# Lightning attention and a SwiGLU FFN in one kernel: an FFN that opens on two blocks, equal weight pieces, and DMA transposes issued with their loads

## The chip, the cores and the metric

The kernel runs on one core of one Trainium2 chip. The metric is device time in microseconds of one execution. Durations of single instructions come from one profiled execution.

## The reference, cut to what matters

There are 4 sequences of 768 tokens, 8 heads of 64, and a decay `lam` per head. Attention is linear with decay; the reference goes over blocks of 64 tokens and carries a state `kv` per head:

```python
intra = (q_b @ k_b.T * Dmask) @ v_b               # inside the block
inter = (q_b * lam_pow) @ kv                      # what came before it
out_b = intra + inter
kv = lam**block * kv + (k_b * rev_pow).T @ v_b
```

The output, seen as x of 3072 tokens by 512, goes through the FFN, with weights of 512 x 1536, 512 x 1536 and 1536 x 512:

```python
g = x @ w_gate
y = (g * sigmoid(g) * (x @ w_val)) @ w_out        # float32, 3072 x 512
```

## The kernel before, in words

**Tiling.** The kernel uses blocks of 128 tokens: 6 per sequence, N = 24 in all. The heads are kept as four pairs (HP), so one block is 128 x 512. The FFN works on tiles of blocks, `TILES`: tile 0 has blocks 0 to 3, tiles 1 and 2 have two blocks each (4 and 5, 6 and 7), and tiles 3 to 6 have four blocks each. The 1536 hidden columns are 12 steps (`fc`) of 128.

**Loads.** `load_kq(n)` loads k and q of a block on the queue of GpSimd (POOL), which turns float32 into bf16 on the way; `load_v(n)` loads v as float32. SyncE (SP) loads lambda, k and q of block 0, and v of the first `FIRST` blocks. Weights w_gate and w_val come in pieces whose widths, in units of 128 columns, are in `PIECES`; `load_w(c)` loads one piece of both, `load_wo(c)` a quarter of w_out. All of them are issued by POOL.

**Attention of a block** is four helpers:
- `scale_v(n)` multiplies v by the reversed decay, on POOL.
- `transposes(n)` gives kT and qT. For n under `PE_T` = 8, TensorE (PE) transposes into PSUM, ScalarE (ACT) copies k, and VectorE (DVE) multiplies q by the decay `qscale`. From block 8 on it is one DMA transpose of k and q together, issued by SP (L184).
- `scores(n)` multiplies kT and qT on PE (L207); DVE multiplies by the mask into `ssb` (L213).
- `cluster(n, n2)` is the rest: the state's part `kv_bd` x qT (L221), then `scores(n2)` if one is named, then `v_s` x `ssb` (L227), the copy into `xT` (L232 on ACT, or L234 on DVE from block 8 on), and the state's update: `up` on PE (L240), `kv_st` on DVE, its bf16 copy `kv_bd` in two halves (ACT for n under `PE_T`, L251; POOL from then on, L253), and `kv_dec`, the decayed state (DVE, then POOL).

**FFN.** `fc_mms(tt, fc, lo, hi)` does the four matmuls of gate and the four of value of one step on the columns lo to hi of a tile (L273). `ffn_fc` adds Silu on ACT (L286) and the product with the value on DVE into `h_sb` (L289). `ffn_out(tt, sub)` does 12 matmuls with w_out for one block (L297), copies on ACT (L300) and stores through SP (L301).

**Buffers that matter.** PSUM pool `ps_f` has 4 buffers, shared by gate, value, PE transposes and, from block 8 on, `up`. `ps_o` has 2 (attention outputs and FFN outputs) and `ps_s` has 1 (scores). Loads of k and q have 10 buffers, v 9, `v_s` 4, `qkT` 6.

**Order.** `tc.manual_schedule()` keeps the order of the program text on every engine, so that each engine is a queue with its instructions in the order in which the helpers are called. POOL issues a DMA when its place in that order comes; in the trace it has at most eight loads of its own under way. `keep_warm` puts matmuls without use into gaps of the opening. In the opening, attention of blocks 0 to 3 is interleaved with loads of weights; then tile 0 opens: its first two steps run on three blocks (`LAST`), while block 3 is finished, and then on the fourth. Blocks 4 to 7 are computed between the steps of tiles 0 and 1. From tile 2 on there is one block for every three steps, in three positions `pos`:

```python
if pos == 0:   scores(8) once; scale_v(n + 1); transposes(n + 3)
elif pos == 1: cluster(n, n + 1)
elif pos == 2: load(n + 6); ffn_out(*outs.pop(0))
```

The FFN outputs run behind: while tile 2 is computed, tile 0 is put out, and four outputs are left for the end.

Of the kernel before, what the change touches and what calls it, by code (L numbers as in the profile page):

```python
# [9 lines left out]
BF16 = mybir.dt.bfloat16  # L10
AF = mybir.ActivationFunctionType
# [11 lines left out]
def kernel(  # L23
# [20 lines left out]
    MC = DM // 128  # L44
    FC = DFF // 128
    TT = 512
    FIRST = 4
    PE_T = 8

    TILES = [(0, 4), (4, 2), (6, 2)] + [(i, 4) for i in range(8, N, 4)]  # L50
    PIECES = [1, 2, 3, 3, 3]
    PIECE_OF = [(c, f) for c, w in enumerate(PIECES) for f in range(w)]
    OPC = 3

# [21 lines left out]
    def load_v(n, eng):  # L76
        b, j = divmod(n, NB)
        v_raw[n] = vpool.tile([128, H, D], FP32, name="v_raw", tag="v_raw")
        eng.dma_start(out=v_raw[n], in_=v5[b, j])  # L79

    def load_kq(n):
        b, j = divmod(n, NB)
        t = ld.tile([128, 2, H, D], BF16, name="kq_nat", tag="kq")
        nc.gpsimd.dma_start(out=t[:, 0], in_=k5[b, j])  # L84
        nc.gpsimd.dma_start(out=t[:, 1], in_=q5[b, j])  # L85
        k_nat[n], q_nat[n] = t[:, 0], t[:, 1]
        state["kq", n] = t

    def load(n):
        load_kq(n)  # L90
        load_v(n, nc.gpsimd)

    wg_sb, wv_sb, wo_sb = {}, {}, {}
    wg_r = moe_w_gate.rearrange("(c p) f -> p c f", p=128)
# [44 lines left out]
                   allow_small_or_imprecise_dtypes=True)  # L139
    causal = const.tile([128, 128], BF16, name="causal")  # L140
    make_upper_triangular(nc, causal, val=1.0, diag=True)
    load_kq(1)
    load_kq(2)

# [13 lines left out]
    lamb = const.tile([128, HP], FP32, name="lamb")  # L158
    nc.scalar.activation(lamb, ln_all[:, H:H + HP], AF.Exp, scale=float(BLK))

    kv_bd = []
    for i in range(2):
        t = const.tile([128, HP, 128], BF16, name=f"kv_bd{i}")
        nc.vector.memset(t, 0.0)
        kv_bd.append(t)
    mask = const.tile([128, 2, HP, BLK], BF16, name="mask")
    nc.vector.tensor_tensor(out=mask, in0=bap(causal, [[0, 2], [0, HP], [1, BLK]]),
                            in1=bap(invb, [[1, 2], [2, HP], [0, BLK]]), op=ALU.mult)
# [47 lines left out]
    def cluster(n, scores_of=None):  # L216
        j = n % NB
        op = ps_o.tile([128, HP, BLK], FP32, name="op", tag="o")
        if j > 0:
            for p in range(HP):  # L220
                nc.tensor.matmul(op[:, p, :], kv_bd[n % 2][:, p, :], qT[n][:, p, :],  # L221
                                 start=(p == 0), stop=False, skip_group_check=True)
        if scores_of is not None:
            scores(scores_of)
        for p in range(HP):
            for h2 in range(2):
                nc.tensor.matmul(op[64 * h2:64 * h2 + 64, p, :], v_s[n][:, 2 * p + h2, :],  # L227
                                 ssb[n][:, h2, p, :], start=(j == 0 and p == 0), stop=(p == HP - 1),
                                 skip_group_check=True)
        x = xT[:, :, n * BLK:(n + 1) * BLK]  # L230
        if n < PE_T:
            nc.scalar.copy(out=x, in_=op)  # L232
        else:
            nc.vector.tensor_tensor(out=x, in0=op, in1=qscale, op=ALU.mult)  # L234
        if j < NB - 1:
            up = (ps_o if n < PE_T else ps_f).tile([128, HP, D], FP32, name="up",
                                                    tag="o" if n < PE_T else "f")
            for p in range(HP):
                for h2 in range(2):
                    nc.tensor.matmul(up[64 * h2:64 * h2 + 64, p, :], k_nat[n][:, 2 * p + h2, :],  # L240
                                     v_s[n][:, 2 * p + h2, :], start=True, stop=True)
            st = apool.tile([128, HP, D], FP32, name="kv_st", tag="kv_st")
            if j == 0:
                nc.vector.tensor_copy(out=st, in_=up)
            else:
                nc.vector.tensor_tensor(out=st, in0=state.pop("dec"), in1=up, op=ALU.add)  # L246
            bd = kv_bd[(n + 1) % 2]
            for h2 in range(2):
                r = slice(64 * h2, 64 * h2 + 64)
                if n < PE_T:  # L250
                    nc.scalar.copy(out=bd[r, :, 64 * h2:64 * h2 + 64], in_=st[r])  # L251
                else:
                    nc.gpsimd.tensor_copy(out=bd[r, :, 64 * h2:64 * h2 + 64], in_=st[r])  # L253
            if j < NB - 2:
                dec = apool.tile([128, HP, D], FP32, name="kv_dec", tag="kv_dec")
                (nc.vector if n < PE_T else nc.gpsimd).tensor_tensor(
                    out=dec, in0=st, in1=bap(lamb, [[1, HP], [0, D]]), op=ALU.mult)
                state["dec"] = dec
        del ssb[n], v_s[n], k_nat[n], kT[n], qT[n]
# [16 lines left out]
            if i == 0 and gate_done is not None:  # L276
                gate_done()

    def ffn_fc(tt, fc, lo=0):
        nt = TILES[tt][1] * BLK  # L280
        if tt not in h_sb:
            h_sb[tt] = hpool.tile([128, FC, TT], BF16, name="h_sb", tag="h")
        sil = fpool.tile([128, TT], BF16, name="sil", tag="sil")

        def silu():
            nc.scalar.activation(sil[:, 0:nt], gv[tt, fc][0][:, 0:nt], AF.Silu)  # L286

        fc_mms(tt, fc, lo, nt, silu)
        nc.vector.tensor_tensor(out=h_sb[tt][:, fc, 0:nt], in0=sil[:, 0:nt],  # L289
                                in1=gv.pop((tt, fc))[1][:, 0:nt], op=ALU.mult)  # L290

    def ffn_out(tt, sub):
        t0 = (TILES[tt][0] + sub) * BLK
        op = ps_o.tile([128, DM], FP32, name="yp", tag="o")
        for fc in range(FC):
            c, f = divmod(fc, OPC)
            nc.tensor.matmul(op, h_sb[tt][:, fc, sub * 128:(sub + 1) * 128], wo_sb[c][:, f, :],  # L297
                             start=(fc == 0), stop=(fc == FC - 1))
        osb = fpool.tile([128, DM], FP32, name="osb", tag="osb")
        nc.scalar.copy(out=osb, in_=op)  # L300
        nc.sync.dma_start(out=out[t0:t0 + 128, :], in_=osb)  # L301


    primed = const.tile([128, HP], FP32, name="primed")
    transposes(0)
    scale_v(0)
    load_kq(3)
    keep_warm(3)
    scores(0)
    scale_v(1)  # L310
    load_w(0)
    keep_warm(5)
    cluster(0)
    transposes(1)
    nc.scalar.activation(primed, lamb, AF.Silu)
    keep_warm(2)
    scores(1)
    scale_v(2)
    load_w(1)
    keep_warm(4)  # L320
    transposes(2)
    cluster(1)
    keep_warm(1)
    scores(2)
    scale_v(3)
    load_w(2)
    keep_warm(4)
    cluster(2)
    transposes(3)
    load_w(3)  # L330
    keep_warm(3)
    scores(3)


    LAST = (FIRST - 1) * BLK
    fc_mms(0, 0, 0, LAST)
    cluster(3)
    fc_mms(0, 1, 0, LAST)
    ffn_fc(0, 0, LAST)
    ffn_fc(0, 1, LAST)  # L340
    load(4)
    load_w(4)
    load(5)
    for fc in range(2, FC):
        ffn_fc(0, fc)
        if fc == 3:
            load(6)
        elif fc == 5:
            load(7)
        elif fc == 7:  # L350
            scale_v(4)
            transposes(4)
            for c in range(2):
                load_wo(c)
        elif fc == 8:
            scores(4)
            scale_v(5)
            for c in range(2, 4):
                load_wo(c)
        elif fc == 9:  # L360
            cluster(4)
            transposes(5)
        elif fc == 10:
            scores(5)
            load(8)


    fc_mms(1, 0, 0, BLK)
# [1 line left out]
    fc_mms(1, 1, 0, BLK)  # L370
    ffn_fc(1, 0, BLK)
    ffn_fc(1, 1, BLK)
    load(9)
    scale_v(6)
    transposes(6)
    for fc in range(2, FC):
        ffn_fc(1, fc)
        if fc == 2:
            scores(6)
            scale_v(7)  # L380
            load(10)
        elif fc == 5:
            transposes(7)
            transposes(8)
        elif fc == 6:
            cluster(6, 7)
            load(11)
            scale_v(8)
        elif fc == 8:
            cluster(7)  # L390
            load(12)
        elif fc == 9:
            transposes(9)
            load(13)
    transposes(10)


    outs = [(0, s) for s in range(4)] + [(1, 0), (1, 1), (2, 0), (2, 1)]
    outs += [(tt, s) for tt in range(3, len(TILES)) for s in range(4)]
    for tt in range(2, len(TILES)):  # L400
        for per in range(4):
            n = 4 * (tt - 2) + 8 + per
            for pos in range(3):
                ffn_fc(tt, 3 * per + pos)
                if pos == 0:
                    if n == 8:
                        scores(8)
                    if n + 1 < N:
                        scale_v(n + 1)
                    if n + 3 < N:  # L410
                        transposes(n + 3)
                elif pos == 1:
                    if n < N:
                        cluster(n, n + 1 if n + 1 < N else None)
                elif pos == 2:
                    if n + 6 < N:
                        load(n + 6)
                    ffn_out(*outs.pop(0))
    for o in outs:
        ffn_out(*o)  # L420
# [31 lines left out]
```

## Time and profile before

| what | value |
|---|---|
| median of 13 runs | 245.65 us (242.23 to 247.16) |
| the profiled execution | 245.0 us; the span of its instructions 243.2 us |
| granted TensorE clock over the span | 0.991 |
| PE, PEld, DVE, ACT, POOL busy | 95%, 50%, 43%, 33%, 46% |
| HBM read, written | 28.32 MB, 6.29 MB |
| a matmul step of 512 columns (8 matmuls) | 1.73 us |
| an output of one block (12 matmuls) | 2.59 us |
| a load of k, of q, of v, issue to landing (medians) | 7.0, 7.5, 8.1 us |
| a DMA transpose, issue to landing (median of 16) | 7.4 us |

The page gives the busy time of each engine, the same in 40 slices of 6.1 us, the DMA queues, the chain of work that ended last, the costliest groups of instructions, and the DMA issues. In a timeline row the columns are start and duration in us, engine, line, operation, output and input, the number of instructions, and in brackets the idle time of the engine before it with what ended it. SPq marks SP's queue, where waiting and issuing count and no work is done. A busy PE is not PE at its peak, since matmuls overlap.

### The profile page before, as it was taken

To read this page: it belongs to the slowest core of one execution; us is meant where nothing else is said; L and a number is where in the kernel's file an instruction comes from. 1 tells how busy PE (TensorE), PEld (TensorE's weight loads), DVE (VectorE), ACT (ScalarE), POOL (GpSimd) and SP (SyncE) were. 2 spreads that over 40 slices of the span, in tenths; PEclk is the share of its full clock that TensorE was granted. 3 is DMA by queue.
4 is the path that set the end of the run, shared out by engine and by line. 5 is a ranking of instruction groups with operands and counts; after the bars stand their busy time and mean duration, and the time that the engine had idled before them with its cause. 6 is when DMAs were issued, how large, how long until landed. Compare 5 with 4: busy or idle time off the path is not lost.

```text
span 243.2 us, 4289 instructions
## 1 busy us (share of the span) xinstructions
PE 230.3 (95%) x1712; PEld 122.7 (50%) x1712; DVE 104.3 (43%) x168; ACT 79.5 (33%) x152; POOL 111.9 (46%) x150
## 2 busy tenths in 40 slices
PE   8898999999299999999999999999999999999993
PEld 3465445787257764455455444445545444444441
DVE  2874545675345543454355256246246322322200
ACT  6565445447002222213213213222221222232121
POOL 8599559999445892745834940331231000000000
PEclk9999999999979999999999999999999999999999
DMA  7999999999999999899779893513100110111022
GB/s 122 194 145 187 207 201 221 203 210 140 157 162 153 185 135 166 165 133 154 74 119 156 93 186 86 67 23 88 46 9 34 46 43 0 43 46 43 24 105 86
DMA packets 83075, 28.32 MB, mean 116 GB/s; under 512 B 73072, under 2 KB 78704, under 8 KB 83056
## 3 DMA queue, kind: packets, MB, share of 16 engines
q0 software_dynamic: 56320, 16.00, 67.6%
q1 hardware_dynamic: 26736, 12.07, 26.7%
q8 instruction: 13, 0.21, 0.4%
q14 instruction: 6, 0.05, 0.1%
HBM read 28.32 MB, written 6.29 MB: 142 GB/s over the span
## 4 chain that ended last, share of the span: by engine, by line
PE 89%; DMA 5%; ACT 2%; DVE 2%; issue 1%; ACTq 0%; DVEq 0%
PE yp L297 26%; PE gp L273 26%; PE vp L273 24%; DMA qkT<-kq_nat 5%; PE op L227 3%; PE sp L207 3%; PE warm_ps L126 2%; PE tp L193 2%; PE op L221 2%; PE up L240 1%; DVE ssb L213 1%; ACT xT L232 1%; ACT kv_bd L251 1%; ACT qkT L195 0%; DVE qkT L196 0%
## 5 line engine op out<-in xcount | busy, mean ns | idle before, releaser
L289 DVE TENSOR_TENSOR h_sb<-sil,vp 128x512 bf16<-128x512 bf16 (+1 forms) x84 | 51.0, 611 | 108.0 <-PE vp L273 92.8
L273 PE MATMUL gp<-xT,wg 128*128 128x512 bf16 (+3 forms) x352 | 77.2, 342 | 0.2
L273 PE MATMUL vp<-xT,wv 128*128 128x512 bf16 (+3 forms) x352 | 77.1, 342 | 0.0
L286 ACT ACTIVATE sil<-gp 128x512 bf16<-128x512 f32 (+1 forms) x84 | 44.7, 536 | 80.6 <-PE gp L273 74.8
L297 PE MATMUL yp<-wo,h_sb 128*128 128x512 bf16 x288 | 66.5, 383 | 0.0
L273 PEld LDWEIGHTS <-wv 128*128 128x128 bf16 x352 | 33.9, 98 | 29.1
L297 PEld LDWEIGHTS <-h_sb 128*128 128x128 bf16 x288 | 28.5, 99 | 34.0 <-issue 1.4
L273 PEld LDWEIGHTS <-wg 128*128 128x128 bf16 x352 | 31.7, 98 | 27.6 <-issue 0.5
L253 POOL CAST kv_bd<-kv_st 64x256 bf16<-64x256 f32 x26 | 10.2, 393 | 63.8 <-DVE kv_st L246 47.7
L300 ACT COPY osb<-yp 128x512 f32<-128x512 f32 x24 | 14.1, 586 | 65.8 <-PE yp L297 65.8
L213 DVE TENSOR_TENSOR ssb<-sp,mask 128x1024 bf16<-128x1024 f32 (+1 forms) x28 | 29.5, 1066 | 7.2 <-PE sp L207 7.0
L177 POOL TENSOR_TENSOR v_s<-v_raw,rev 128x512 bf16<-128x512 f32 x24 | 25.6, 1070 | 3.2 <-DMA v_raw<-in_v_dram 3.0
L84 POOL DMA_DIRECT2D kq_nat<-in_k_dram x23 | 21.4, 932 | 2.1 <-DMA kq_nat<-in_k_dram 1.2
L85 POOL DMA_DIRECT2D kq_nat<-in_q_dram x23 | 20.5, 893 | 2.6 <-DMA wg<-in_moe_w_gate_dram 1.5
L79 POOL DMA_DIRECT2D v_raw<-in_v_dram x20 | 18.2, 912 | 2.9 <-DMA kq_nat<-in_k_dram 2.2
L207 PE MATMUL sp<-qkT 64*128 64x128 bf16 x192 | 9.5, 219 | 7.0 <-DMA qkT<-kq_nat 5.0
L207 PEld LDWEIGHTS <-qkT 64*128 64x128 bf16 x192 | 5.5, 94 | 12.4 <-DMA qkT<-kq_nat 5.4
L126 PE MATMUL warm_ps<-warm 128*128 128x512 bf16 x32 | 10.4, 459 | 1.2 <-DVE warm L121 1.2
L234 DVE TENSOR_TENSOR xT<-op,qscale 128x512 bf16<-128x512 f32 x16 | 10.9, 681 | 0.0
L227 PE MATMUL op<-ssb,v_s 128*64 128x128 bf16 x192 | 10.1, 225 | 0.5 <-DVE ssb L213 0.5
L221 PE MATMUL op<-qkT,kv_bd 128*128 128x128 bf16 x80 | 7.7, 219 | 0.3 <-ACT kv_bd L251 0.3
L227 PEld LDWEIGHTS <-v_s 128*64 128x64 bf16 x192 | 6.1, 109 | 3.5 <-POOL v_s L177 0.7
(47 smaller groups left out, 89.5 us busy)
## 6 DMA issues: line engine op xcount, KB each, us to landing
out_dram<-osb SPq DMA_DIRECT2D x24, 256.0 KB, 2.2
v_raw<-in_v_dram POOLq DMA_DIRECT2D x20, 256.0 KB, 8.1
kq_nat<-in_k_dram POOLq DMA_DIRECT2D x23, 128.0 KB, 7.0
kq_nat<-in_q_dram POOLq DMA_DIRECT2D x23, 128.0 KB, 7.5
wo<-in_moe_w_out_dram POOLq DMA_DIRECT2D x4, 384.0 KB, 7.4
wg<-in_moe_w_gate_dram POOLq DMA_DIRECT2D x3, 384.0 KB, 7.7
wv<-in_moe_w_val_dram POOLq DMA_DIRECT2D x3, 384.0 KB, 8.9
v_raw<-in_v_dram SPq DMA_DIRECT2D x4, 256.0 KB, 7.4
```

Of the source, the lines that this page charges most:

```text
L79: eng.dma_start(out=v_raw[n], in_=v5[b, j])
L84: nc.gpsimd.dma_start(out=t[:, 0], in_=k5[b, j])
L85: nc.gpsimd.dma_start(out=t[:, 1], in_=q5[b, j])
L126: nc.tensor.matmul(warm_ps, warm[:, 0:128], warm, start=True, stop=True)
L177: nc.gpsimd.tensor_tensor(out=t, in0=v_raw.pop(n), in1=bap(rev, [[1, H], [0, D]]), op=ALU.mult)
L207: nc.tensor.matmul(sp[:, h2, p, :], kT[n][r, p, :], qT[n][r, p, :], start=True, stop=True)
L213: nc.vector.tensor_tensor(out=s[:, :, ps], in0=sp[:, :, ps], in1=mask[:, :, ps], op=ALU.mult)
L227: nc.tensor.matmul(op[64 * h2:64 * h2 + 64, p, :], v_s[n][:, 2 * p + h2, :], ssb[n][:, h2, p, :], start=(j == 0 and p == 0), stop=(p == HP ...
L273: nc.tensor.matmul(gv[tt, fc][i][:, lo:hi], w[c][:, mc, fs], xT[:, mc, t0 + lo:t0 + hi], start=(mc == 0), stop=(mc == MC - 1))
L286: nc.scalar.activation(sil[:, 0:nt], gv[tt, fc][0][:, 0:nt], AF.Silu)
L289: nc.vector.tensor_tensor(out=h_sb[tt][:, fc, 0:nt], in0=sil[:, 0:nt], in1=gv.pop((tt, fc))[1][:, 0:nt], op=ALU.mult)
L297: nc.tensor.matmul(op, h_sb[tt][:, fc, sub * 128:(sub + 1) * 128], wo_sb[c][:, f, :], start=(fc == 0), stop=(fc == FC - 1))
```

## The change

- `FIRST` becomes 3, so SP loads v of blocks 0 to 2 only; k, q and v of block 3 are loaded by POOL between weight pieces. The weight pieces become six of 256 columns.
- The zeroing of `kv_bd` moves from DVE to POOL, ahead of POOL's first load. The Silu table is loaded (`primed`) before block 1's transposes instead of after them.
- Tile 0 opens after scores(2): step 0 on blocks 0 and 1, then cluster(2), then step 1 on two blocks, then both on block 2; steps 2 to 5 on three blocks, with block 3's attention between them; then steps 0 to 5 on block 3 alone, and steps 6 to 11 on all four. `ffn_fc` gets a range of columns for this.
- For blocks from 8 on, `load` issues the DMA transpose right after the loads, so SP's queue has the transposes in the order of the loads. Loads are called four blocks ahead of the cluster instead of six, and `transposes` is no longer called three blocks ahead.
- In tile 2 the four clusters stand at other places: scores(8) after the first output, cluster(8) after step 3, cluster(9) after the second output, cluster(10) after step 7, cluster(11) after step 10. `scale_v` and the loads follow the clusters.
- Stores of the output are issued by ACT instead of SP.
- The bf16 copies of the state for blocks 8 to 11 go from POOL to ACT.

```diff
-    FIRST = 4
+    FIRST = 3
-    PIECES = [1, 2, 3, 3, 3]
+    PIECES = [2] * 6
 def load(n):
     load_kq(n)
     load_v(n, nc.gpsimd)
+    if n >= PE_T:
+        transposes(n)
...
+    for i in range(2):                      # ahead of load_kq(1), load_kq(2)
+        t = const.tile([128, HP, 128], BF16, name=f"kv_bd{i}")
+        nc.gpsimd.memset(t, 0.0)            # was nc.vector.memset, later
...
-                if n < PE_T:
+                if n < 12:
                     nc.scalar.copy(out=bd[r, :, 64 * h2:64 * h2 + 64], in_=st[r])
...
-        nc.sync.dma_start(out=out[t0:t0 + 128, :], in_=osb)
+        nc.scalar.dma_start(out=out[t0:t0 + 128, :], in_=osb)
```

The opening and tile 2, as they stand after the change:

```python
transposes(0); scale_v(0); load_w(0); keep_warm(3); scores(0)
scale_v(1); load_w(1); keep_warm(4); cluster(0)
nc.scalar.activation(primed, lamb, AF.Silu); keep_warm(4)
transposes(1); scale_v(2); load(3); keep_warm(2); scores(1)
load_w(2); keep_warm(2); transposes(2); cluster(1)
load_w(3); keep_warm(1); scores(2)
A, B3 = 2 * BLK, 3 * BLK
fc_mms(0, 0, 0, A); cluster(2); fc_mms(0, 1, 0, A)
ffn_fc(0, 0, A, B3); ffn_fc(0, 1, A, B3)
scale_v(3); load_w(4); ffn_fc(0, 2, 0, B3); load_w(5)
transposes(3); ffn_fc(0, 3, 0, B3); load(4)
scores(3); ffn_fc(0, 4, 0, B3); load(5)
cluster(3); ffn_fc(0, 5, 0, B3); load(6)
for fc in range(6):
    ffn_fc(0, fc, B3, 4 * BLK, B3)
for fc in range(6, FC):
    ffn_fc(0, fc)          # after 8: scale_v(4), load(7); after 9: transposes(4), scale_v(5)
...                        # after 10: scores(4), transposes(5), load_wo(0), load_wo(1)
cluster(4); scores(5)
...                        # tile 1: load(8) after step 2, load(9) after 5, load(10) after 8, load(11) after 10
for per in range(4):                       # tile 2
    for pos in range(3):
        ffn_fc(2, 3 * per + pos)
        if pos == 2:
            ffn_out(*outs.pop(0))
        if (per, pos) == (0, 2):
            scores(8)
        elif (per, pos) == (1, 0):
            cluster(8, 9); scale_v(10); load(12)
        elif (per, pos) == (1, 2):
            cluster(9, 10); scale_v(11); load(13)
        elif (per, pos) == (2, 1):
            cluster(10, 11); scale_v(12); load(14)
        elif (per, pos) == (3, 1):
            cluster(11, 12); scale_v(13); load(15)
```

In tiles 3 to 6 the cluster stays at position 1, now with `scale_v(n + 2)` and `load(n + 4)` right behind it, and the output at position 2.

More of the change, by code (lines that the diff above doesn't have):

```diff
@@ L141 @@
     make_upper_triangular(nc, causal, val=1.0, diag=True)
+    kv_bd = []
+    for i in range(2):
+        t = const.tile([128, HP, 128], BF16, name=f"kv_bd{i}")
+        nc.gpsimd.memset(t, 0.0)
+        kv_bd.append(t)
     load_kq(1)
@@ L159 @@
     nc.scalar.activation(lamb, ln_all[:, H:H + HP], AF.Exp, scale=float(BLK))
[L161 to L165, printed above, removed]
     mask = const.tile([128, 2, HP, BLK], BF16, name="mask")
@@ L277, in fc_mms, with ffn_fc @@
                 gate_done()
-    def ffn_fc(tt, fc, lo=0):
-        nt = TILES[tt][1] * BLK
+    def ffn_fc(tt, fc, lo=0, hi=None, frm=0):
+        hi = TILES[tt][1] * BLK if hi is None else hi
         if tt not in h_sb:
@@ L283, in ffn_fc @@
         sil = fpool.tile([128, TT], BF16, name="sil", tag="sil")
+        cs = slice(frm, hi)
         def silu():
[L286 to L290, printed above, removed]
+            nc.scalar.activation(sil[:, cs], gv[tt, fc][0][:, cs], AF.Silu)
+        fc_mms(tt, fc, lo, hi, silu)
+        nc.vector.tensor_tensor(out=h_sb[tt][:, fc, cs], in0=sil[:, cs],
+                                in1=gv.pop((tt, fc))[1][:, cs], op=ALU.mult)
     def ffn_out(tt, sub):
@@ L306 @@
     scale_v(0)
-    load_kq(3)
+    load_w(0)
     keep_warm(3)
@@ L310 @@
     scale_v(1)
-    load_w(0)
-    keep_warm(5)
+    load_w(1)
+    keep_warm(4)
     cluster(0)
+    nc.scalar.activation(primed, lamb, AF.Silu)
+    keep_warm(4)
     transposes(1)
-    nc.scalar.activation(primed, lamb, AF.Silu)
+    scale_v(2)
+    load(3)
     keep_warm(2)
     scores(1)
-    scale_v(2)
-    load_w(1)
-    keep_warm(4)
+    load_w(2)
+    keep_warm(2)
     transposes(2)
     cluster(1)
+    load_w(3)
     keep_warm(1)
     scores(2)
+    A, B3 = 2 * BLK, 3 * BLK
+    fc_mms(0, 0, 0, A)
+    cluster(2)
+    fc_mms(0, 1, 0, A)
+    ffn_fc(0, 0, A, B3)
+    ffn_fc(0, 1, A, B3)
     scale_v(3)
-    load_w(2)
-    keep_warm(4)
-    cluster(2)
+    load_w(4)
+    ffn_fc(0, 2, 0, B3)
+    load_w(5)
     transposes(3)
-    load_w(3)
-    keep_warm(3)
+    ffn_fc(0, 3, 0, B3)
+    load(4)
     scores(3)
-    LAST = (FIRST - 1) * BLK
-    fc_mms(0, 0, 0, LAST)
+    ffn_fc(0, 4, 0, B3)
+    load(5)
     cluster(3)
[L338 to L344, printed above, removed]
+    ffn_fc(0, 5, 0, B3)
+    load(6)
+    for fc in range(6):
+        ffn_fc(0, fc, B3, 4 * BLK, B3)
+    for fc in range(6, FC):
         ffn_fc(0, fc)
-        if fc == 3:
-            load(6)
-        elif fc == 5:
+        if fc == 8:
+            scale_v(4)
             load(7)
-        elif fc == 7:
-            scale_v(4)
+        elif fc == 9:
             transposes(4)
-            for c in range(2):
-                load_wo(c)
-        elif fc == 8:
+            scale_v(5)
+        elif fc == 10:
             scores(4)
[L357 to L361, printed above, removed]
             transposes(5)
-        elif fc == 10:
-            scores(5)
-            load(8)
+            load_wo(0)
+            load_wo(1)
+    cluster(4)
+    scores(5)
     fc_mms(1, 0, 0, BLK)
@@ L372 @@
     ffn_fc(1, 1, BLK)
-    load(9)
     scale_v(6)
-    transposes(6)
+    load_wo(2)
+    load_wo(3)
     for fc in range(2, FC):
@@ L378 @@
         if fc == 2:
+            transposes(6)
+            scale_v(7)
+            load(8)
+        elif fc == 3:
             scores(6)
-            scale_v(7)
-            load(10)
         elif fc == 5:
             transposes(7)
-            transposes(8)
+            load(9)
         elif fc == 6:
             cluster(6, 7)
-            load(11)
             scale_v(8)
@@ L390 @@
             cluster(7)
[L391 to L395, printed above, removed]
+            load(10)
+        elif fc == 10:
+            load(11)
+            scale_v(9)
     outs = [(0, s) for s in range(4)] + [(1, 0), (1, 1), (2, 0), (2, 1)]
     outs += [(tt, s) for tt in range(3, len(TILES)) for s in range(4)]
-    for tt in range(2, len(TILES)):
+    for per in range(4):
+        for pos in range(3):
+            ffn_fc(2, 3 * per + pos)
+            if pos == 2:
+                ffn_out(*outs.pop(0))
+            if (per, pos) == (0, 2):
+                scores(8)
+            elif (per, pos) == (1, 0):
+                cluster(8, 9)
+                scale_v(10)
+                load(12)
+            elif (per, pos) == (1, 2):
+                cluster(9, 10)
+                scale_v(11)
+                load(13)
+            elif (per, pos) == (2, 1):
+                cluster(10, 11)
+                scale_v(12)
+                load(14)
+            elif (per, pos) == (3, 1):
+                cluster(11, 12)
+                scale_v(13)
+                load(15)
+    for tt in range(3, len(TILES)):
         for per in range(4):
-            n = 4 * (tt - 2) + 8 + per
+            n = 4 * tt + per
             for pos in range(3):
                 ffn_fc(tt, 3 * per + pos)
[L405 to L414, printed above, removed]
+                if pos == 1 and n < N:
+                    cluster(n, n + 1 if n + 1 < N else None)
+                    if n + 2 < N:
+                        scale_v(n + 2)
+                    if n + 4 < N:
+                        load(n + 4)
                 elif pos == 2:
-                    if n + 6 < N:
-                        load(n + 6)
                     ffn_out(*outs.pop(0))
```

## The prediction

> **What bounds the kernel now.** I read the page first (busy shares, slices, the chain of work that ended last), then the waits, then the timeline around the two places where TensorE (PE) stands still.
>
> ```profile
> PE   8898999999299999999999999999999999999993
> PEclk9999999999979999999999999999999999999999
> PE 89%; DMA 5%; ACT 2%; DVE 2%; issue 1%; ACTq 0%; DVEq 0%
> ```
>
> PE carries 89% of the chain: nearly all the rest of the kernel is matmuls back to back, and only idle PE time can be won. The one large hole is the slice marked 2 (61 to 67 us), with the only clock digit under 9 right behind it. The share of 5% for DMA names the cause; cut into stages by hand:
>
> ```profile
> 16.00:20.05 4.05, 2.90 (x42) 1.68 (x40) 2.38 (x5) 2.18 (x5) 4.05 (x7) 1.00 1.25 148
> 20.05:44.36 24.31, 24.30 (x189) 12.83 (x185) 12.99 (x20) 10.91 (x20) 18.97 (x24) 1.00 1.57 205
> 44.36:60.84 16.48, 15.94 (x201) 13.05 (x199) 10.04 (x22) 9.32 (x22) 16.35 (x19) 1.00 1.60 182
> 60.84:68.20 7.36, 2.41 (x45) 1.90 (x46) 2.35 (x4) 0.38 (x1) 2.64 (x3) 1.00 1.77 152
> ```
>
> Columns: stretch, length, then busy us of PE, PEld, DVE, ACT, POOL, granted clock, DMA share. Tile 0 of the FFN (20.05 to 44.36) is full; 60.84 to 68.20 has 2.41 us of matmul in 7.36, so **4.95 us idle**. The timeline names who ends it:
>
> ```profile
> 53.12 14.64 SPq L184 DMA_TRANSPOSE qkT<-kq_nat  x4
> 62.38 0.40 PE L207 MATMUL sp<-qkT 64*128 64x128 bf16 x8 [1.54 <-DMA qkT<-kq_nat]
> 67.39 0.40 PE L207 MATMUL sp<-qkT 64*128 64x128 bf16 x8 [3.41 <-DMA qkT<-kq_nat]
> ```
>
> scores(8) and scores(9) wait for the first two DMA transposes (1.54 + 3.41 = 4.95). I call the transpose of block n T(n) and its loads L(n). T8 is issued at 53.12, as soon as q of block 8 has landed (44.23 + 8.8 us to landing), and takes 9.2 us more; T9 takes 11.7, T10 12.5, T11 11.5, T12 7.8. The DMA row of the page is at 9 from the second slice to the sixteenth, so the rings are a queue and what is late is late by its place in it.
>
> The other place is the start:
>
> ```profile
> 2.06 1.07 POOL L84 DMA_DIRECT2D kq_nat<-in_k_dram  x1
> 12.33 1.28 ACT L315 ACT_TABLE_LOAD   x1
> 12.37 0.40 PE L207 MATMUL sp<-qkT 64*128 64x128 bf16 x8 [1.01 <-ACT qkT L195]
> 19.72 0.40 PE L207 MATMUL sp<-qkT 64*128 64x128 bf16 x8 [0.85 <-ACT qkT L195]
> 20.05 0.82 PE L273 MATMUL gp<-xT,wg 128*128 128x384 bf16 x4
> ```
>
> The first FFN matmul runs at 20.05, behind scores(3).
>
> **What the skill says.** "TensorE: Matmul & The Clock Gate" (Part 1) says that an idle window of some 3.4 us puts the PE clock to half. The trace agrees in kind: after the waits of 1.54 and 3.41 us the granted clock averages 0.86 over 68 to 80 us, 12 x 0.14 = **1.7 us** lost. "DMA: Bandwidth & Descriptors" (Issuing engines are not separate DMA queues) says that moving a DMA to another issuing engine saves only issue time; the trace shows SP's v loads and POOL's k and q loads landing in turn, so stores on ACT cost the rings what they did. "Perfetto Trace Analysis" (DMA Instruction — HWDGE) says that one descriptor generator serves both hardware-issuing engines under a lock. Before, only SP uses it; no run here shows it contended. I use it for a rival.
>
> **The change, part by part.** Loads land in order. In the saturated stretch k, q and v follow each other by some 0.9 us, a weight piece of 384 columns takes 1.9, of 256 columns 1.3, a piece of w_out 1.95.
>
> *Start.* The two memsets of kv_bd go from VectorE (DVE, 0.55 us for both, hidden there) to POOL, ahead of its first load. POOL's 128x128 memset took 0.20 and a one-column one 0.10; four times the columns gives an estimate of 0.5 each, so POOL's first load starts at 3.1 instead of 2.1. v of block 3 leaves SP's queue, which gives back the same 1 us of ring: q of block 1 lands near 10, of block 2 near 12.7, in time for their transposes. The Silu table load moves ahead of the copy of qkT(1): ACT finishes kv_bd near 11.6, then 1.28 + 0.20 + 0.59, so scores(1) runs at 13.7 instead of 12.4, 1.3 later. transposes(2) and cluster(1) follow (ssb(1) done at 15.4), scores(2) at 15.9, and the FFN opens on 256 columns at **16.3**. Weight piece 0 (issued after scale_v(0), near 8.8) lands by 15.5 (two transfers of 1.3 behind q of block 2).
>
> From there PE must do what it did before from 20.05 to 44.36 (24.1 us of work) and also cluster(2) 0.95, transposes(3) 0.45, scores(3) 0.33: 25.8. New waits: cluster(2) for ssb(2), 0.45; the 12 extra activations and products of 128 columns in the catch-up (0.44 us of PE per step, the 256-column row of ACT 0.38 and of DVE 0.42 against two pairs of buffers), 0.5; buffers 0.1. Tile 1 opens at 16.3 + 26.9 = **43.2** instead of 44.36: gain **1.15**. The 128-column matmuls cost no more per column (four took 0.22, four of 512 took 0.86). Covers: piece 1 lands 17.8 for 20.3, piece 2 23.4 for 24.3, k and q of block 3 20.0 for 21.6, its v 20.9 (scaled 22.0) for 25.2, pieces 3 to 5 with 4 us and more.
>
> *The hole.* Bytes ahead of T8 are the same, so T8 is issued near 51.5. Its user is moved back: scores(8) stood after the first step of tile 2, now after three steps and the first output (two steps of 0.87 and 2.59 later). PE is there at 43.2 + 16.5 + 1.74 + 2.59 = **64.0**. With T8's 9.2 us it lands by 60.7. The hole goes: **4.95** won, and the clock behind it, **1.5** of the 1.7.
>
> *What is late next.* Tile 2 now runs its four clusters within 16 us, two of them (after step 6 and at step 8) with no output between. Needed times: T9 65.6, T10 71.2, T11 74.1, T12 80.5. With before's spacing (5 us, then 4 to 6) T9 lands near 65, T10 69, T11 74. L12 stands on POOL behind kv_dec(8), that is behind cluster(8) on PE and kv_st on DVE: issued 69, q landed near 74.6, T12 with 7.8 us at **82.5**. And the states: kv_bd of blocks 8 to 11 goes from POOL (0.84 for both halves) to ACT (0.83), in order ahead of the next activations; it waits for kv_st on DVE, which comes after ssb (1.22) and xT (0.68). An activation is held some 2 us, the pairs of buffers run out: 0.6 at the first cluster, 0.6 + 0.4 at the second: **1.6**, which also moves T12's need to 81.5 or more. Stall for T12 **1.0**, clock behind it **0.3**. From both sides: nothing at all if T12 is in time; 8 and more in the rival below.
>
> *Stores on ACT.* 24 issues at SP's 0.34 us: 8.2 us of ACT, which is 33% busy. In tiles of 512 columns the activation after a store may be 1.8 us late before a buffer is missing; in tile 2 some 0.4. Hidden, unless the issue is longer than on SP. SP has then only transposes; nothing stands behind their waits. Tiles 3 to 6 keep their order of PE work; loads go four blocks ahead and land with 9 us and more to spare: nothing.
>
> *Sum* against the profiled execution (245.0; span 243.2, 1.8 around it): -1.15 - 4.95 - 1.5 + 1.6 + 1.0 + 0.3 = -4.7; span 238.5, time 240.3. The median of the runs, 245.65, is 0.65 above that execution, so I say **240.9**.
>
> **Rivals.**
> - *Likeliest, 0.58*: as summed; own range 238.5 to 243.5.
> - *The transposes are in time, 0.17*: without the 1.3 for T12 and most of the 1.6: 238.2. For it: only two blocks of loads, not three, are queued when T8 starts.
> - *The wait comes back at T12, slower, 0.17.* One mechanism: L12 is tied to cluster(8), and T12 to L12. Against loads and stores in flight q at 80.55 took 8.8 us and the transpose at 81.02 10.1 us. Then T12 lands at 69.7 + 8.8 + 10.1 = 88.6, 7.1 late even with its need at 81.5; T9 to T11 lag 2 more, the states 1.6, the clock 1.7: 12.4 lost against 7.6 won: 250.4 at the worst. It decides from T12 near 85 (the gain is gone when some 7.6 us are lost in all); slower by a measurable amount from 86 to 87, 247 there.
> - *ACT waits for the descriptor generator, 0.08.* Transposes held it 1.2 to 4.6 us at 53 to 67. A store behind one of 4.6 stops the activations; two such in tile 2 cost 2 x 2.5: 245 to 246. Against it: the late transposes took 1.3 to 1.6, less than the slack of tiles 3 to 6.
> - *The start wins nothing*: if the table load or w pieces hold the opening to 17.5, 1.15 goes: 242.1; inside the likeliest range.
>
> **How the numbers follow.** A difference under about 0.5% (1.2 us) can't be told from none here. Faster takes the first two cases nearly whole: 0.75. Same (244.4 to 246.9) takes the edge of the first, most of the fourth and some of the third: 0.09. Slower: 0.16. Range 237.0 to 247.5: from no loss in tile 2 with a better start, into the third case.
>
> **What would show it.** Right: first FFN matmul near 16.3, tile 1 near 43, no DMA wait ahead of scores(8), a wait of 1 us ahead of scores(12), clock of 1.00 around 66 to 73. Wrong: a DMA wait of more than 3 us ahead of scores(9) to scores(13) (third case); ACT's store issues of over 1 us with PE gaps behind (fourth); an opening later than 18 (start).

## The result, and the profile after

The changed kernel takes 239.89 us (median of 11 runs, 239.55 to 241.53) against 245.19 us (median of 48 runs of the kernel before). The ratio is 0.9816, with a 95% interval of 0.979 to 0.9842, so it is some 1.8% faster. Medians here and below count every execution, while ratios leave out those that took over 1.5% longer than the fastest of the same kernel. The profiled execution has a span of 237.6 us, where it was 243.2.

The same rows of the page as before, from the profile of the changed kernel: PE's slices, the granted clock, the chain.

```profile
PE   7879999999998999999999999999999999999993
...
PEclk9999999999999999999999999999999999999999
...
PE 84%; ACT 6%; DMA 4%; DVE 3%; issue 2%; ACTq 0%
```

The slice marked 2 is gone, and so is the low clock digit behind it. Stretches of the changed kernel (stretch, length, busy us of PE, PEld, DVE, ACT, POOL, granted clock, DMA share, GB/s): tile 0 with the catch-up, tile 1 to the first output, tile 2's four clusters.

```profile
16.24:43.31 27.07, 26.63 (x273) 17.06 (x269) 15.96 (x32) 13.86 (x31) 24.12 (x29) 1.00 1.62 194
43.31:61.54 18.23, 17.55 (x217) 14.66 (x217) 11.68 (x23) 10.72 (x26) 13.91 (x16) 1.00 1.51 186
61.54:82.42 20.88, 19.53 (x199) 12.76 (x197) 11.09 (x19) 7.10 (x18) 12.09 (x14) 1.00 1.19 136
```

Tile 2 has 1.35 us of idle PE where 60 to 70 us held 4.95. What ended its waits, from the timeline of PE (start, duration, line, and in brackets the idle time and its releaser):

```profile
64.22 0.40 PE L209 MATMUL sp<-qkT 64*128 64x128 bf16 x8
...
65.94 0.40 PE L209 MATMUL sp<-qkT 64*128 64x128 bf16 x8
...
68.58 0.60 PE L275 MATMUL vp<-xT,wv 128*128 128x256 bf16 x4 [0.36 <-DVE kv_st L248]
...
74.57 0.60 PE L275 MATMUL vp<-xT,wv 128*128 128x256 bf16 x4 [0.36 <-DVE kv_st L248]
...
75.42 0.40 PE L223 MATMUL op<-qkT,kv_bd 128*128 128x128 bf16 x4 [0.26 <-ACT kv_bd L253]
...
82.42 0.40 PE L209 MATMUL sp<-qkT 64*128 64x128 bf16 x8 [0.26 <-DMA qkT<-kq_nat]
```

scores(8) and scores(9) have no bracket: they wait for nothing. scores(12) waits 0.26 us for T12. The opening, from the timeline of the changed kernel:

```profile
2.05 0.98 POOL L147 MEMSET kv_bd<- 128x512 bf16 x2
...
11.42 1.28 ACT L318 ACT_TABLE_LOAD   x1
...
13.45 0.40 PE L209 MATMUL sp<-qkT 64*128 64x128 bf16 x8 [1.58 <-ACT qkT L197]
...
16.24 0.61 PE L275 MATMUL gp<-xT,wg 128*128 128x256 bf16 x4
```

The FFN opens at 16.24, and scores(1) has waited 1.58 us for the copy behind the table load.

### The profile page after: what moved, and what is told of

Same layout as the page of the kernel before. It is cut to its first block, busy times and chain, and to the rows that moved or that the text cites. A ratio compares the mean times of both kernels' runs of the same rounds, so it can differ in the third digit from the quotient of the medians.

```text
span 237.6 us, 4385 instructions
## 1 busy us (share of the span) xinstructions
PE 227.8 (96%) x1754; PEld 123.7 (52%) x1754; DVE 104.9 (44%) x171; ACT 82.9 (35%) x164; POOL 112.4 (47%) x149
## 4 chain that ended last, share of the span: by engine, by line
PE 84%; ACT 6%; DMA 4%; DVE 3%; issue 2%; ACTq 0%
PE yp L301 25%; PE gp L275 25%; PE vp L275 24%; PE op L229 3%; PE sp L209 3%; DMA qkT<-kq_nat 2%; ACT kv_bd L253 2%; PE op L223 2%; DVE ssb L215 2%; ACT xT L234 1%; DMA lam_all<-in_lam_dram 1%; PE tp L195 1%; PE up L242 1%; ACT sil L290 1%; ACT L318 1%
## 5 line engine op out<-in xcount | busy, mean ns | idle before, releaser
L293 DVE TENSOR_TENSOR h_sb<-sil,vp 128x512 bf16<-128x512 bf16 (+3 forms) x90 | 51.7, 580 | 103.4 <-PE vp L275 89.0
L290 ACT ACTIVATE sil<-gp 128x512 bf16<-128x512 f32 (+3 forms) x90 | 45.4, 512 | 68.7 <-PE gp L275 67.9
L301 PE MATMUL yp<-wo,h_sb 128*128 128x512 bf16 x288 | 65.4, 379 | 0.0
L275 PEld LDWEIGHTS <-wv 128*128 128x128 bf16 x376 | 35.2, 98 | 28.8 <-issue 1.3
L275 PEld LDWEIGHTS <-wg 128*128 128x128 bf16 x376 | 33.2, 98 | 26.4 <-issue 1.1
L255 POOL CAST kv_bd<-kv_st 64x256 bf16<-64x256 f32 x20 | 7.9, 394 | 49.7 <-DVE kv_st L248 34.3
L79 POOL DMA_DIRECT2D v_raw<-in_v_dram x21 | 19.4, 922 | 0.0
L253 ACT CAST kv_bd<-kv_st 64x256 bf16<-64x256 f32 x20 | 8.1, 403 | 8.7 <-DVE kv_st L248 7.5
L258 POOL TENSOR_TENSOR kv_dec<-kv_st,lamb 128x256 f32<-128x256 f32 x10 | 6.1, 608 | 9.6 <-DVE kv_st L248 8.9
L128 PE MATMUL warm_ps<-warm 128*128 128x512 bf16 x26 | 8.6, 465 | 1.2 <-DVE warm L123 1.2
```

Of the source, the lines that this page charges most:

```text
L275: nc.tensor.matmul(gv[tt, fc][i][:, lo:hi], w[c][:, mc, fs], xT[:, mc, t0 + lo:t0 + hi], start=(mc == 0), stop=(mc == MC - 1))
L290: nc.scalar.activation(sil[:, cs], gv[tt, fc][0][:, cs], AF.Silu)
L293: nc.vector.tensor_tensor(out=h_sb[tt][:, fc, cs], in0=sil[:, cs], in1=gv.pop((tt, fc))[1][:, cs], op=ALU.mult)
```

## The experiments

As in the prediction, T8 is the DMA transpose of block 8 and L8 its loads. My theory: DMA transposes are slow when block loads run beside them, that is, are issued and not yet landed, and what the change wins is the end of the wait for T8 and T9. Rivals: the later places of their users in tile 2 win it; or the opening does; or T8 is slowed by the transposes behind it and not by loads (experiment 8 bears on that).

**1. The opening alone.** The kernel before with `FIRST = 3`, `PIECES = [2] * 6`, zeroing on POOL, early table load and the new text up to tile 1; the rest as before.

> The kernel before with the new opening alone (six equal pieces, FFN on two blocks, zeroing on POOL, table load early); from tile 1 on as before, DMA transposes, stores and states too. Theory (the transposes of blocks 8 and 9 are set by the DMA rings, not by PE): tile 1 opens near 43.3 instead of 44.4, but scores(8) then waits the longer for T8, which still lands near 62; 244.5 to 245.5 us, no gain that can be told. Rival (the opening's gain counts by itself): 243.9 to 244.2 us, 1.1 less than before.

Measured: 245.63 us, ratio 1.002 (0.9992 to 1.0048). Tile 1 opens at 43.61, and T8 still takes 9.2 us:

```profile
61.83 0.40 PE L207 MATMUL sp<-qkT 64*128 64x128 bf16 x8 [1.34 <-DMA qkT<-kq_nat]
...
66.28 0.40 PE L207 MATMUL sp<-qkT 64*128 64x128 bf16 x8 [2.85 <-DMA qkT<-kq_nat]
```

A hole of 4.2 us is there, and by itself the opening moves nothing that can be told from zero.

**2. The rest alone.** The changed kernel with the opening of before.

> The changed kernel with the opening of before (pieces of 1, 2, 3, 3, 3, FFN on three blocks). Theory: no hole ahead of scores(8) and scores(9), clock 1.00; only the 1.1 us of the opening are missing: 240.8 to 241.3 us. Rival (the opening carries more than its 1.1, since it also frees the rings earlier): 242.5 us and more, with a DMA wait at scores(9) or scores(12) of over 1.5 us.

Measured: 239.73 us, ratio 0.9798 (0.9748 to 0.9848); the changed kernel's 0.9816 lies inside that interval. So the rest gives all of the gain; my 1.1 us for the opening did not show even here, where nothing of the DMA eats it. The trace tells why. Tile 1 opens at 43.98 in this run and at 43.31 to 43.68 in four runs with the new opening (after and experiments 1, 4 and 5). Then tile 1 up to the first output takes 17.82 us here and 18.23 with the new opening, which puts cluster(4) right ahead of tile 1, so that the first step waits 0.23 us for xT and cluster(5) 0.24 for the state.

**3. One line in the kernel before.** POOL must have v of block 8 before it issues L10:

```diff
         if fc == 2:
             scores(6)
             scale_v(7)
-            load(10)
...
         elif fc == 6:
             cluster(6, 7)
-            load(11)
             scale_v(8)
+            load(10)
+            load(11)
```

> The kernel before with one edit: load(10) is called behind scale_v(8) instead of ahead of it, so POOL, waiting for v of block 8, holds L10 and L11 back until L8 has landed. Theory A (T8 is slow because two or three blocks of loads run beside it): T8 takes 5 to 6 us instead of 9.2 and lands by 59, no wait ahead of scores(8), under 1.5 ahead of scores(9); 240 to 242 us. Theory B (what counts is that the users of T8 and T9 stand later in the changed kernel): T8 lands after 61, waits of over 3 us stay, 244 us or more.

Measured: 238.4 us (four runs, 238.1 to 238.9), ratio 0.9747 (0.9697 to 0.9797). The places in tile 2 are those of before, and so are kv_bd on POOL and the stores on SP. In the kernel before, POOL issues L10 first and comes to scale_v(8) later, with nothing left to wait for:

```profile
50.61 0.95 POOL L84 DMA_DIRECT2D kq_nat<-in_k_dram  x1
...
56.09 1.05 POOL L177 TENSOR_TENSOR v_s<-v_raw,rev 128x512 bf16<-128x512 f32 x1
```

From the trace of this run:

```profile
52.80 10.04 SPq L184 DMA_TRANSPOSE qkT<-kq_nat  x3
...
54.77 0.95 POOL L84 DMA_DIRECT2D kq_nat<-in_k_dram  x1
...
60.58 0.40 PE L207 MATMUL sp<-qkT 64*128 64x128 bf16 x8
...
62.40 0.40 PE L207 MATMUL sp<-qkT 64*128 64x128 bf16 x8 [0.22 <-DMA qkT<-kq_nat]
```

L10 starts at 54.77, where it started at 50.61 before; T8 takes 5.6 us instead of 9.2, and the hole of 4.95 is 0.22. The span falls by 6.5 us (243.2 to 236.7): 4.7 of waits, and the 1.7 of low clock behind them. Theory A stands: the loads beside the transposes made the hole, and neither the later places nor the new opening is needed to close it. None of its four runs is as slow as the fastest of the changed kernel (239.55) or of experiment 2 (239.42).

**4. The places of before in the changed kernel.** scores(8) after step 0, clusters at position 1.

> The changed kernel with the places of before in tile 2: scores(8) after step 0, one cluster after step 1 of each three; loads and transposes as changed. Theory A (loads that no longer crowd the transposes are what removes the hole): T8 lands near 57.7, before scores(8) at 59.8; T9 near 61.7, a wait of 0.5 us at most; the waits of 0.36, 0.36, 0.26 and 0.26 us in tile 2 go; 239.0 to 239.8 us, as fast as the changed kernel or 0.5 faster. Theory B (the later places are needed): waits of 2 us or more ahead of scores(8) to scores(10), 242 us and up.

Measured: 238.41 us, ratio 0.9753 (0.9707 to 0.9799). The profiled execution (239.56; the four others 238.26 to 238.45) has a wait of 1.45 ahead of scores(9), against the 0.5 that I expected, and none of tile 2's other waits. With the loads held, the new places win nothing; if anything they cost about 1 us.

**5. The changed kernel again**, as base for the next three.

> The changed kernel as it is, on the same chip as the three that follow, as their base: 239.5 to 240.1 us.

Measured: 240.13 us, ratio 0.9822 (0.9781 to 0.9862).

**6. No hold on POOL.** The undoing of experiment 3, in the changed kernel:

```diff
             cluster(6, 7)
-            scale_v(8)
...
             load(11)
+            scale_v(8)
             scale_v(9)
```

> The changed kernel with scale_v(8) called behind load(11), so that POOL issues L10 and L11 without waiting for v of block 8. Theory A (loads beside a transpose make it slow): T8 takes 8 us or more again and lands near 61 to 62, T9 near 66; scores(8) at 64.2 does not wait, scores(9) and scores(10) wait up to 2 us together; 240 to 242 us. Theory B (T8's duration has to do with SP's queue or with stores): T8 still takes 5 us, no new wait, 239.9 us.

Measured: 240.74 us, ratio 0.9832 (0.9792 to 0.9872). T8 lands 9.1 us after its issue, where it was 5.0 in the changed kernel:

```profile
L186 SPq DMA_TRANSPOSE qkT<-kq_nat x1: 1351/1351/1351, 53.4 to 53.4; - x1
DMA to landing us min/median/max: 9.1/9.1/9.1
```

scores(8) waits for nothing, and scores(9) 0.89. The ratio lies only 0.001 above that of experiment 5, and the intervals overlap, so the time decides nothing; T8's duration does. The later places take up most of the wait that would come back. The changed kernel thus has two remedies, of which either would do most.

**7. States of blocks 8 to 11 on POOL**, as before: `n < PE_T` in place of `n < 12`.

> The changed kernel with the bf16 states of blocks 8 to 11 on POOL, as before. Prediction's view (ACT's in-order hold of the activations is what runs the PSUM pairs out): the waits of 0.36, 0.36 and 0.26 us in tile 2 shrink to under 0.4 in all, 239.2 us. Rival (it is kv_st on DVE, behind ssb and xT, that keeps the buffer of up): the 0.36 us stay, and POOL's copy, behind three DMA issues of 0.9 us, makes cluster(10) wait 1 us or more: 240 to 241 us.

Measured: 240.0 us, ratio 0.9807 (0.9771 to 0.9842), as the base. Each side was half right. Both waits of 0.36 go, so ACT's hold made them, though the trace names kv_st as their end; which buffer the value matmul waited for was not settled. In exchange POOL's copy is late, and T12 later behind it:

```profile
75.33 0.40 PE L223 MATMUL op<-qkT,kv_bd 128*128 128x128 bf16 x4 [0.91 <-POOL kv_bd L255]
...
82.84 0.40 PE L209 MATMUL sp<-qkT 64*128 64x128 bf16 x8 [0.77 <-DMA qkT<-kq_nat]
```

**8. T8 earlier**, on experiment 4: `load(8)` with its transpose ahead of `load_wo(0)`.

> The kernel of e4_old_places with load(8) and with it its transpose called ahead of the four pieces of w_out. Theory (the transposes come late by their place in the rings, so what the opening won on PE is lost at scores(8) and scores(9)): T8 is issued near 44.5 and lands before 52, T9 before 61; no DMA wait ahead of scores(8) to scores(10); w_out lands by 56, 8 us before its use; 237.0 to 238.0 us. Rival (the transposes drag on w_out and L9, T9 stays near 63): a wait of 1 to 2 us ahead of scores(9), 238.4 us or more.

Measured: 245.08 us, ratio 1.001 (0.9985 to 1.0035). My theory of a place in the queue falls, and with it the prediction's "late by its place"; the rival was right, by more than it said. T8 is issued at 44.43 and takes 13.1 us among the pieces of w_out, L9 and L10. No other DMA transpose runs beside it, so it does not take one to make T8 slow. L9's k lands at 57.79, 10.8 us after its issue (9.2 in experiment 4), so T9 is issued at 58.47 only. The edit also undid the hold: v of block 8 is there early, scale_v(8) at 49.71 waits for nothing, and L10 starts at 50.70 instead of 56.04.

```profile
65.07 0.61 PE L209 MATMUL sp<-qkT 64*128 64x128 bf16 x8 [3.22 <-DMA qkT<-kq_nat]
```

This wait is 1.8 us longer than the one of experiment 4, but the span is 4.7 us longer (242.2 for 237.5). The rest is the clock: it is 0.50 from 65 to 71 us.

**9. Only cluster(8, 9) later**, on experiment 4: behind tile 2's first output.

> The kernel of e4_old_places with only cluster(8, 9) moved behind the first output of tile 2 (3.5 us of PE work later); the other clusters at the places of before. Theory (places of before cost only the wait for T9, the places of the changed kernel cost the pairs' waits of 1.3 us): T9 near 63.3 for a need near 64.5, no DMA wait over 0.3 us, PE idle from 60 to 90 us under 0.4; 237.0 to 238.0 us, 2 us under the changed kernel. Rival (T10, behind it, is now what comes late, since cluster(9, 10) follows 4 us later): a wait of 1 us or more ahead of scores(10), 238.4 us or more.

Measured: 240.55 us (238.62 to 242.91), ratio 0.9777 (0.9717 to 0.9838), no gain over experiment 4 that can be told. There is no wait ahead of scores(9) or scores(10), but L12 is called behind cluster(8): T12 is issued 1.2 us later than in experiment 4 and takes 8.5 us instead of 5.1, with more loads beside it, and scores(12) waits 1.56 us for it. Waits of 0.36 and 0.26 us around cluster(9) are back too. The rival had the mechanism and named the wrong block.

**10. Stores on SP**, on experiment 9: `nc.sync.dma_start` in `ffn_out`.

> e9_cluster8_later with the stores on SP's queue, as before the change. Theory (store issues on ACT are hidden, and on SP they only stand behind transposes that wait for their loads): within 0.3 us of e9_cluster8_later. Rival (ACT's 0.34 us per store delays activations, or the generator is shared): 1 us or more faster than it; the other way round, if stores behind waiting transposes hold up the buffers of the output: 1 us or more slower.

Measured: 239.67 us (238.98 to 240.26), ratio 0.9758 (0.9713 to 0.9802); not to be told from experiment 9.

**11. The table load late**, on experiment 9: `primed` behind `transposes(1)`.

> e9_cluster8_later with the Silu table loaded after the copies of block 1's transposes, as before the change. Theory of the prediction (the early load costs 1.3 us at scores(1)): scores(1) at 12.3, FFN opening at 15.6 instead of 16.5, tile 1 at 42.8, and of it 0.5 us or more in the end, since T8 and T9 have little to spare. Rival (the table load then stands ahead of the copy of block 2's kT and costs the same there): opening at 16.2 or later, no change.

Measured: 239.53 us (237.78 to 241.99), ratio 0.9741 (0.9685 to 0.9797); not to be told from experiment 9. Its profiled execution is the slowest of the six (241.99): scores(12) waits 2.00 us in it, and from 84 to 87 us the clock is 0.50. So only the opening is read from it:

```profile
12.87 0.40 PE L209 MATMUL sp<-qkT 64*128 64x128 bf16 x8 [0.20 <-ACT qkT L197]
...
15.66 0.61 PE L275 MATMUL gp<-xT,wg 128*128 128x256 bf16 x4
```

scores(1) comes 0.86 us earlier than in experiment 9, and so does the FFN (15.66 for 16.52). The cost of the early table load is real; whether it reaches the end stays open.

**12. The transposes nearly alone**, on experiment 9:

```diff
             transposes(7)
-            load(9)
         elif fc == 6:
             cluster(6, 7)
             scale_v(8)
+            load(9)
         elif fc == 8:
             cluster(7)
+            scale_v(9)
             load(10)
```

(and `scale_v(9)` goes from behind load(11)).

> e9_cluster8_later with load(9) held behind scale_v(8) and load(10) behind scale_v(9), so that T8 runs with hardly a load beside it and T9 with at most one block. Theory (a transpose is slow by what runs beside it): T8 takes 3 to 4 us from issue to landing (5 us with one block of loads beside it, 9 with two to three), T9 4 to 5 us; 237.0 to 238.0 us. Rival (5 us is what a transpose takes): T8 still 5 us or more, and T9 and T10 later by what the loads were held, waits of 1 us or more ahead of scores(9) or scores(10), 238.5 us or more.

Measured: 245.29 us, ratio 1.0022 (0.9984 to 1.0061). The duration came as the theory said:

```profile
L186 SPq DMA_TRANSPOSE qkT<-kq_nat x1: 1365/1365/1365, 52.8 to 52.8; - x1
DMA to landing us min/median/max: 3.1/3.1/3.1
```

The time came as the rival said: each block's loads now wait for the block before, T9 is issued at 60.15 and T10 at 67.25, and PE stands:

```profile
72.92 0.61 PE L209 MATMUL sp<-qkT 64*128 64x128 bf16 x8 [3.90 <-DMA qkT<-kq_nat]
```

Behind this wait the clock is 0.50 from 73 to 76 us.

**The traces together.** T8 from issue to landing, by the loads that were under way beside it (three loads make a block; the average is worked out from the times of issue and landing in the traces):

| runs | loads beside T8, on average | T8, us |
|---|---|---|
| 12 | 0.7 | 3.1 |
| after, 2 to 5, 7, 9 to 11 | 2.7 to 3.4 | 4.1 to 5.7 |
| 6 | 5.2 | 9.1 |
| before, 1 | 6.9, 7.3 | 9.2 |
| 8 | 6.3, pieces of w_out among them | 13.1 |

That fewer loads make T8 faster is shown: in 8 and in 12 no other DMA transpose runs beside it, and it takes 13.1 and 3.1 us. Their number gives only a rough order, and whether it is their number, their bytes or their kind that counts was not tested.

## Why the prediction was right

**The hole went, as forecast, and the clock with it.** 4.95 us of waits became none at scores(8) and scores(9), and the granted clock over 68 to 80 us rose from 0.86 to 1.00.

**But the step that explained it was mis-sized.** I carried T8's 9.2 us over and let the later place of scores(8), at 64.0, cover it. PE was at scores(8) at 64.22, as worked out, and T8 had landed at 57.7: issued at 52.70 (1.2 us later than I said), it took 5.0 us. T8 before the change, and after it:

```profile
L184 SPq DMA_TRANSPOSE qkT<-kq_nat x1: 1342/1342/1342, 53.1 to 53.1; - x1
DMA to landing us min/median/max: 9.2/9.2/9.2
...
L186 SPq DMA_TRANSPOSE qkT<-kq_nat x1: 1354/1354/1354, 52.7 to 52.7; - x1
DMA to landing us min/median/max: 5.0/5.0/5.0
```

I had named the cause only in the second case (two blocks of loads queued instead of three, 0.17) and did not see what enforces it. In the changed order scale_v(8) stands ahead of load(10), and POOL waits there. From the timeline of the changed kernel:

```profile
53.97 1.04 POOL L179 TENSOR_TENSOR v_s<-v_raw,rev 128x512 bf16<-128x512 f32 x1 [4.15 <-DMA v_raw<-in_v_dram]
54.96 0.94 POOL L84 DMA_DIRECT2D kq_nat<-in_k_dram  x1
```

A wait of 4.15 us on an engine that issues loads, harmless for PE, is what clears the way for T8. Experiments 3 and 6 show it from both sides. The later places would have served too: in experiment 6, with T8 at 9.1 us, they leave 0.89 us of the 4.95. So the mechanism that I argued would have been enough; what closed the hole here came before it, since T8 was early.

**The opening** was right in its times (FFN at 16.24 for 16.3, tile 1 at 43.31 for 43.2, memsets 0.98 for 1.0, scores(1) at 13.45 for 13.7), and its term was wrong. 1.15 us was taken against one execution's 44.36; three executions with the old opening (before, experiments 2 and 3) open tile 1 at 43.98 to 44.36, so 0.6 is the mean difference, and 0.4 of it goes back in tile 1, a step that I left out. In the time nothing of it is seen (experiments 1 and 2).

**Tile 2**: T12 landed at 82.37 (82.5 said) and cost 0.26 instead of 1.0. The states cost 0.98 (0.36, 0.36, 0.26) instead of 1.6; that they move the waits and do not add them was not foreseen (experiment 7).

**The stores** were hidden, as said, as far as experiment 10 can tell. **The rival of the late T12** did not decide here, but experiments 8, 9 and 12 show its kind: transposes that come late cost 1.6 to 3.9 us at one place, and in 8 and 12, with the low clock behind the wait, the whole gain.

The sum, -4.7 us of span, came out at -5.6. Tile 2 lost 1.24 us instead of the 2.9 forecast (1.6 + 1.0 + 0.3), and the opening gave less than its 1.15; these errors have opposite signs, so that the sum came so close is in part luck. The measured 239.89 lies between the likeliest case (240.9) and the second one (238.2), in which the transposes are in time.

## What to carry to other kernels

When a DMA is late, look at what runs beside it before asking for it earlier: asking earlier (experiment 8) put it into worse company. A load that nobody needs yet can be held back by an instruction of the issuing engine that waits for data anyway; one such line gave here as much as a new order of the opening, of tile 2 and of the stores together. More holding is not better: in the order of before, the kernel takes 245 us with some seven loads beside T8 and 238.4 with some three; in experiment 12, where each block's loads wait for the block before, it takes 245 again.

## What was not expected of the hardware

A wait of PE cost more than itself once it was long. The granted clock was 0.50 for 3.4 us after a wait of 2.00 us (experiment 11) and one of 3.90 (12), after 1.54 and 3.41 (before) and after 1.34 and 2.85 (1), and for 6.8 us after one of 3.22 (8). That is another 1.5 to 1.7 us lost, and some 3.1 in experiment 8. After waits of up to 1.59 us with no longer one behind them it stayed at 1.00. The prediction speaks of an idle window of some 3.4 us; here, in one execution, 2.00 was enough.

The same 256 KB transpose in SBUF takes 3.1 to 13.1 us from issue to landing, by what else is under way. The Trainium skill ("DMA: Bandwidth & Descriptors", Rules for kernel authors) says that a transpose next to ordinary DMAs "needs nothing"; that is said of correctness, and for time the runs here show otherwise.
